# Another closing order for a gated linear attention and mixture-of-experts kernel on one core

## The chip, the core and the metric

The kernel runs on one NeuronCore of a Trainium2 chip. The metric is the time of one execution in microseconds, as the device measures it. The engines are TensorE (PE in the profile; PEld is its weight load and PEq or PEldq its sequencer), VectorE (DVE), ScalarE (ACT), GpSimd (POOL) and SyncE (SP). Each has its own instruction stream; they meet at semaphores. A name with q behind it (SPq, ACTq) is that engine's sequencer, which issues DMAs, reads registers and takes branches.

## The reference, cut

```python
f = 1.0 / (1.0 + np.exp(-f_logit))                  # q, k, v, f_logit: 4 x 8 x 768 x 48
for t in range(S):
    state = f[:, :, t, :, None] * state + np.einsum('bhd,bhe->bhde', k[:, :, t], v[:, :, t])
    y[:, :, t] = np.einsum('bhd,bhde->bhe', q[:, :, t], state)
x = y.transpose(0, 2, 1, 3).reshape(3072, 384)
P = np.exp(x @ w_gate - max); 8 rounds of row and column normalisation
for e in range(8):
    out += P[:, e:e + 1] * (np.maximum(x @ w1[e], 0.0) @ w2[e])   # w1: 384 x 1024, w2: 1024 x 384
```

## The kernel before

`fast` computes everything on the assumption that the inputs lie in ranges for which its scaled 16-bit arithmetic holds. It also computes a flag (`guard`, `verdict`) that says whether they do. `tile_gla_moe` reads the flag into a register of every engine after `fast` (line 271), and a branch (`tc.If(bad > 0)`, line 272) runs the slow program `general` when it is set. Here it never is: the branch jumps over `general`.

After the attention and the first two experts comes the long main part: 48 periods, `ORDER[n] = (e, m, b)`, the expert, the half of its hidden units and the batch. Every operand is split into two 16-bit parts (names ending in h and l), so that each product is three matmuls. Within a period 15 first-layer products (`SLOTS`) go to six PSUM banks called A to F. A bank's life is a list of events (`EVENTS`), run by `event`: `hh`/`hl` make the two parts of a hidden tile (`kh`, `kl`), `ga`/`gf` those of another (`kah`, `kal`), `gs` adds a bank into the sums `kr` and `kf` on VectorE, `gd` subtracts on GpSimd, `gh` rounds a sum to 16 bits on ScalarE (`kgh`) and `gl` makes the low part (`kgl`) on GpSimd.

The second layer is done by `paired(n, h, t)`, one block for each period and each third t of its tokens. A block is a generator that is advanced a step at a time. Its numbered steps, where "product" is six matmuls of 192 columns:

- s1: two products, into y0 and x1 (operands `ka` and the first `kg` tile)
- s2: ScalarE copies y0 to x0, and x1 times a scale to `part`
- s3: one product into y0 (second `kg` tile); s4: ScalarE copies y0 to x1
- s5: one product into x0 (operand `kh`); s7: one into x1 (first `kg` tile); s6 is empty
- s8: VectorE adds one half of each of the two outputs
- s9: two products, into y0 (`kh`) and x1 (second `kg` tile); s10: VectorE adds the other halves, GpSimd adds into `acc`, and the finished rows are stored by a DMA

y0 and x1 are the halves of one PSUM tile p, x0 lies in another tile q. The second `kg` tile of t = 2 has one buffer, which the next period's `gh` with (2, 1) writes again. In the last period ("direct" blocks) GpSimd adds `part` into `acc` at s2, and the results are added straight into `acc`.

The order on the engines is written out by hand: `pin` chains the instructions of ACT, DVE and POOL in the order in which Python emits them, and `mm` does the same for the matmuls. Behind the last first-layer product (into bank F) there remain the half-done block n=46, t=1 and four whole ones: n=46, t=2, and n=47, t=0, 1, 2. Below they are called blocks 139 to 143. `going` holds them as numbers 0 to 4. The tuple `CLOSING` is the order of what is left: a number advances that block by a step, a tuple is an event, `'v'` advances `verdict`. `ENDX` names the PSUM banks of the four whole blocks.

`verdict` has five steps left in `CLOSING`: a transpose on TensorE (`gd_t`), a maximum on VectorE (line 913), a second transpose (`gd_s`), three tiny VectorE instructions (lines 919 to 921), and two more that write the flag (lines 923 and 924).

Of the kernel before, what the change touches and what calls it, by code (L numbers as in the profile page):

```python
# [8 lines left out]
F32 = mybir.dt.float32  # L9
# [10 lines left out]
C = 64  # L20
# [62 lines left out]
READDAT = (9, 14)  # L83
CHECKAT = (1, 5)
MAXAT = (2, 6)
ENDX = (('x', None), ('k0', None), ('x', 'B'), ('k2', None))
CLOSING = (('add', 'C', '+', 3), ('gd', 1, 'P'), ('gh', 0, 1), 0, 1, 0, ('hh', 'D', 2), 0, ('gl', 0, 0), ('gl', 0, 1), 1,
# [5 lines left out]
BY_VECTOR = ((0, 0), (1, 0), (2, 0), (2, 1))  # L93
ORDER = [(e, m, b) for e in range(2, NE) for m in range(2) for b in range(B)]
PAIRED = (0, 1, 2)
BY_POOL = (1,)
# [169 lines left out]
def tile_gla_moe(tc, qkf, vc, vt, wg, w1, w2, out):  # L266
    nc = tc.nc
    with tc.tile_pool(name="fl", bufs=1) as fp:
        flag = fp.tile([1, 1], I32, name="flag")
        fast(tc, qkf, vc, wg, w1, w2, out, flag)  # L270
        bad = nc.values_load(flag, min_val=0, max_val=1)
        with tc.If(bad > 0, label="general"):
            general(tc, qkf, vt, wg, w1, w2, out)


# [1 line left out]
def fast(ctx, tc, qkf, vc, wg, w1, w2, out, flag):  # L277
# [615 lines left out]
    def verdict():  # L893
        g = cst.tile([128, 7], F32, name="wg7")
        xm = xmx.rearrange("p b k -> p (b k)")
        pin(nc.vector.tensor_reduce(out=g[:, 2:4], in_=wmx, axis=AX.X, op=ALU.min))
        pin(nc.vector.tensor_reduce(out=g[:, 4:6], in_=wmx, axis=AX.X, op=ALU.max))
        pin(nc.vector.tensor_reduce(out=g[:, 1:2], in_=xm, axis=AX.X, op=ALU.min))
        pin(nc.vector.tensor_reduce(out=g[:, 6:7], in_=xm, axis=AX.X, op=ALU.max))
        yield  # L900
        pin(nc.vector.tensor_scalar(out=okm[:, 1:2], in0=g[:, 2:3], scalar1=W1_MIN / W1S, scalar2=None, op0=ALU.is_ge))
        pin(nc.vector.tensor_scalar(out=okm[:, 2:3], in0=g[:, 3:4], scalar1=W2_MIN / W2S, scalar2=None, op0=ALU.is_ge))
        pin(nc.vector.tensor_scalar(out=okm[:, 3:4], in0=g[:, 5:6], scalar1=W2_MAX / W2S, scalar2=None, op0=ALU.is_le))
        pin(nc.vector.tensor_reduce(out=g[:, 0:1], in_=okm, axis=AX.X, op=ALU.min))
        yield
        pin(nc.vector.tensor_scalar(out=g[:, 0:2], in0=g[:, 0:2], scalar1=-1.0, scalar2=None, op0=ALU.mult))
        pin(nc.vector.tensor_scalar(out=g[:, 2:3], in0=g[:, 2:3], scalar1=-BALANCE, scalar2=None, op0=ALU.mult))
        yield
        ps = pk.tile([128, 128], F32, name="gd_t", tag="D")
        mm(transpose=True, out=ps[0:7, :], in_=g, identity=identf)  # L910
        yield
        col = cst.tile([7, 1], F32, name="gd_c")
        pin(nc.vector.tensor_reduce(out=col, in_=ps[0:7, :], axis=AX.X, op=ALU.max))
        yield
        ps = pk.tile([128, 128], F32, name="gd_s", tag="k1")
        mm(transpose=True, out=ps[0:1, 0:7], in_=col, identity=identf[0:7, 0:7])
        yield
        r = cst.tile([1, 9], F32, name="gd_r")
        pin(nc.vector.tensor_scalar(out=r[:, 0:7], in0=ps[0:1, 0:7], scalar1=1.0, scalar2=None, op0=ALU.mult))
        pin(nc.vector.tensor_tensor(out=r[:, 7:8], in0=r[:, 4:5], in1=r[:, 6:7], op=ALU.mult))  # L920
        pin(nc.vector.scalar_tensor_tensor(out=r[:, 8:9], in0=r[:, 1:2], scalar=r[:, 2:3], in1=r[:, 7:8], op0=ALU.mult, op1=ALU.is_ge))
        yield
        pin(nc.vector.scalar_tensor_tensor(out=r[:, 7:8], in0=r[:, 7:8], scalar=XW1_MAX / W1S, in1=r[:, 0:1], op0=ALU.is_le, op1=ALU.mult))
        pin(nc.vector.tensor_scalar(out=flag, in0=r[:, 8:9], scalar1=r[:, 7:8], scalar2=-FLAG_AT, op0=ALU.mult, op1=ALU.is_gt))
# [289 lines left out]
    first = {b: min(n for n, p in enumerate(ORDER) if p[2] == b) for b in range(B)}  # L1214
    final = {b: max(n for n, p in enumerate(ORDER) if p[2] == b) for b in range(B)}

    def paired(n, h, t, tag="x", own=None):
        e, m, b = ORDER[n]
        new = n == first[b]
        if new and t == PAIRED[0]:  # L1220
            acc[b] = accp.tile([128, 2, TT, DM], F32, name=f"acc{b}", tag="acc")
        p = (pk if own else psm).tile([128, DM], F32, name=f"kyps_{n}_{t}", tag=own or "m")
        q = pk.tile([128, DM], F32, name=f"kxps_{n}_{t}", tag=tag)
        x0, y0, x1 = q[:, 0:DH], p[:, 0:DH], p[:, DH:DM]
        p2 = lp.tile([128, DH], F32, name=f"part_{n}_{t}", tag="part", bufs=2)
        by_pool = t in BY_POOL and n < len(ORDER) - 1 and not new
        xx, yy = (acc[b][:, v, t, :].rearrange("p (s d) -> p s d", s=2) for v in range(2))
        direct = n == len(ORDER) - 1
        if not new and not direct:
# [4 lines left out]
        def scale(v):  # L1234
            return pes[:, (2 * b + v) * TT + t, e:e + 1]
# [27 lines left out]

        def store(v, half):
            r0, ds = (2 * b + v) * HS + t * 128, slice(0, DM) if half is None else slice(half * DH, half * DH + DH)
            (nc.scalar if direct and v else nc.sync).dma_start(out=out[r0:r0 + 128, ds], in_=acc[b][:, v, t, ds])

        product(y0, None, (0, 0), start=True)
        product(x1, (None, 0), (None, 0))
        yield  # L1270
        move(x0, y0)
        move(p2, x1, scale=scale(1))
        if direct:
            for i in range(2):
                pin(nc.gpsimd.tensor_tensor(out=yy[:, i, :], in0=yy[:, i, :], in1=p2, op=ALU.add))
        yield
# [6 lines left out]
        yield  # L1283
        product(x1, (None, 1), (None, 1))
        yield
        out_x(0, x0)
        add(yy[:, 1, :], x1, scale(1), yy[:, 1, :] if direct else p2)
        halved = direct and t == PAIRED[-1]
        if halved:
            for v in range(2):  # L1290
                store(v, v)
        yield
# [5 lines left out]
        for v, z, there in ((0, xx, not by_pool), (1, yy, new or direct)):  # L1298
            if not there:
                y = acc[b][:, v, t, :]  # L1300
                pin(nc.gpsimd.tensor_tensor(out=y, in0=y, in1=z.rearrange("p s d -> p (s d)"), op=ALU.add))  # L1301
            if n == final[b]:
                store(v, 1 - v if halved else None)

    def readds():
        todo = {b: [(o, v, t) for t in range(TT) for v in range(2) for o in range(2) if (o, 2 * b + v) in RAW] for b in range(B)}
# [62 lines left out]
    def event(ctxt, ev):  # L1369
# [45 lines left out]
        elif kind == 'gb':  # L1415
            ah, al = hs['a', ev[1]]
            pin((nc.gpsimd if ev[2] == 'P' else nc.vector).tensor_tensor(out=al, in0=hs['r', ev[1]][:, 0], in1=ah, op=ALU.subtract))
        elif kind == 'gh':
            _, t, i = ev
            if not i:  # L1420
                if t == 2:
                    hs['g', t] = [[hp.tile([128, 2, 2, 128], F16, name=f"kg{q}{i}_{tag}_{t}", tag=f"k{q}1{0}{i}", bufs=1) for i in range(2)] for q in "hl"]
                else:
                    hs['g', t] = [[lp.tile([128, 2, 2, 128], F16, name=f"kg{q}{i}_{tag}_{t}", tag=f"kg{q}{t}{i}", bufs=1) for i in range(2)] for q in "hl"]
            pin(nc.scalar.activation(out=hs['g', t][0][i], in_=hs['f' if i else 'r', t], func=AF.Copy))  # L1425
        elif kind == 'gl':
            _, t, i = ev
            pin((nc.vector if tag == str(PERIODS - 1) and (t, i) in BY_VECTOR else nc.gpsimd).tensor_tensor(out=hs['g', t][1][i], in0=hs['f' if i else 'r', t], in1=hs['g', t][0][i], op=ALU.subtract))  # L1428
        elif kind == 'hh':
            pin(nc.scalar.activation(out=hs['h', ev[2]][0], in_=bk, func=AF.Relu))  # L1430
        else:
            hh, hl = hs['h', ev[2]]
            pin(nc.vector.scalar_tensor_tensor(out=hl, in0=bk, scalar=0.0, in1=hh, op0=ALU.max, op1=ALU.subtract))
# [56 lines left out]
        raise RuntimeError("an event was left")  # L1490

    def close(what):
        if what == 'v':
            next(judged, None)
        elif isinstance(what, tuple):
            event(ctxt, what)
        else:
            next(going[what], None)

    hint = CLOSING.index('hint')  # L1500
    for what in CLOSING[:hint]:
        close(what)
    with tc.block():
        tc.mark_branch_hint_location("general", "LikelyTaken", [mybir.EngineType.DVE, mybir.EngineType.Activation, mybir.EngineType.SP])
        for what in CLOSING[hint + 1:]:
            close(what)
    if any(next(block, going) is not going for block in going):
        raise RuntimeError("a block was left")
    for _ in judged:
# [46 lines left out]
```

## Time and profile before

| | |
|---|---|
| median of 3 runs | 1458.15 us (1458.13 to 1458.2) |
| the profiled execution's own time | 1458.26 us |
| its span, first to last instruction | 1456.4 us |
| TensorE busy, share of the span | 99% |
| VectorE, ScalarE, GpSimd | 85%, 73%, 72% |
| mean granted TensorE clock | 0.999 of full speed |

The span is 1.86 us shorter than the time of the same execution; that remainder lies outside the instructions. Times in the rows below count from the span's start. Behind an instruction, in brackets, stands how long its engine had been idle before it and what ended the wait. The chain of work that ended last is empty in this profile, so the end is followed by hand, engine by engine.

### The profile page before, as it was taken

The page shows a single profiled execution, that of the slowest core. Times are in us where ns is not written, and L with a number is a line of the kernel's source. Part 1 is how long each engine was busy: PE and PEld are TensorE (multiplying, and loading weights), DVE is VectorE, ACT ScalarE, POOL GpSimd, SP SyncE. Part 2 cuts the span into 40 slices and gives each one's busy share as a digit, 9 for nine tenths or more (in the row PEclk, how much of TensorE's full clock was granted, in tenths as well). Part 3 has the DMA queues.
Part 4 walks back from the last instruction along what each step waited for, and adds up shares of the span by engine and source line. Part 5 has one row for each costly group of instructions (what it writes and reads, how often), then busy time and mean ns, then how long its engine had stood idle before and what let it go on. Part 6 is the DMA issues. An engine that isn't in the chain of part 4 may idle for free.

```text
span 1456.4 us, 40359 instructions
## 1 busy us (share of the span) xinstructions
PE 1438.7 (99%) x16054; PEld 1256.4 (86%) x16054; DVE 1232.9 (85%) x2512; ACT 1061.1 (73%) x2382; POOL 1045.1 (72%) x1227
## 2 busy tenths in 40 slices
PE   8999999999999999999999999999999999999997
PEld 5888876666666899999999999999999999999997
DVE  8888788885787899888899999888889888888876
ACT  7766666663354877888888888888877787778764
POOL 4344434446429576999999999999988888888764
PEclk9999999999999999999999999999999999999999
DMA  9455455541011101122212111111111110000012
GB/s 282 122 136 128 117 133 129 118 117 32 29 33 38 35 23 35 51 57 62 61 56 61 51 50 49 46 45 51 50 34 34 34 34 23 17 18 13 2 53 82
DMA packets 105271, 92.58 MB, mean 64 GB/s; under 512 B 72080, under 2 KB 91920, under 8 KB 105072
## 3 DMA queue, kind: packets, MB, share of 16 engines
q1 hardware_dynamic: 104496, 89.32, 22.7%
q8 instruction: 127, 2.08, 0.6%
q14 instruction: 72, 0.59, 0.1%
q10 hardware_dynamic: 576, 0.59, 0.1%
HBM read 64.03 MB, written 14.16 MB: 54 GB/s over the span
## 4 chain that ended last, share of the span: by engine, by line


## 5 line engine op out<-in xcount | busy, mean ns | idle before, releaser
L305 PEld LDWEIGHTS <-k1h 128*128 128x128 f16 x2880 | 270.9, 98 | 21.5 <-issue 2.9
L305 PE MATMUL kyps<-k2h,kgh 128*128 128x192 f16 x1152 | 283.4, 246 | 0.2 <-ACT part L1251 0.2
L305 PE MATMUL kyps<-k2l,kgh 128*128 128x192 f16 x1152 | 283.4, 246 | 0.0
L305 PE MATMUL kyps<-k2h,kgl 128*128 128x192 f16 x1152 | 283.4, 246 | 0.0
L305 PEld LDWEIGHTS <-kgh 128*128 128x128 f16 x2304 | 212.0, 98 | 6.7 <-issue 0.4
L1428 POOL TENSOR_TENSOR kgl<-kf,kgh 128x512 f16<-128x512 f32 x143 | 190.4, 1331 | 1.5 <-ACT kgh L1425 1.5
L1428 POOL TENSOR_TENSOR kgl<-kr,kgh 128x512 f16<-128x512 f32 x141 | 175.1, 1242 | 10.8 <-ACT kgh L1425 10.6
L1254 DVE SCALAR_TENSOR_TENSOR yy<-kyps,pes,part 128x192 f32<-128x192 f32 x258 | 106.7, 414 | 88.5 <-PE kyps L305 78.1
L1301 POOL TENSOR_TENSOR acc<-acc,yy 128x384 f32<-128x384 f32 x129 | 129.5, 1004 | 57.4 <-DVE yy L1254 57.4
L305 PEld LDWEIGHTS <-k1l 128*128 128x128 f16 x1440 | 140.9, 98 | 16.3
L305 PE MATMUL yps<-w2h,hl 128*128 128x384 f16 x384 | 125.1, 326 | 0.5 <-DVE hl L477 0.5
L305 PE MATMUL yps<-w2h,hh 128*128 128x384 f16 x384 | 125.1, 326 | 0.1
L305 PE MATMUL yps<-w2l,hh 128*128 128x384 f16 x384 | 125.1, 326 | 0.0
L305 PEld LDWEIGHTS <-w1h 128*128 128x128 f16 x1344 | 96.9, 98 | 32.0 <-ACT w1h L373 0.4
L305 PEld LDWEIGHTS <-kh 128*128 128x128 f16 x1152 | 108.2, 98 | 7.0 <-issue 0.6
L305 PEld LDWEIGHTS <-kgl 128*128 128x128 f16 x1152 | 112.7, 98 | 0.2 <-issue 0.2
L305 PEld LDWEIGHTS <-hh 128*128 128x128 f16 x768 | 73.6, 98 | 44.2 <-issue 0.5
L1251 ACT ACTIVATE kyps<-kyps 128x192 f32<-128x192 f32 x144 | 45.7, 317 | 80.0 <-PE kyps L305 78.5
L1425 ACT ACTIVATE kgh<-kf 128x512 f16<-128x512 f32 x144 | 91.8, 638 | 0.5 <-DVE kf L1402 0.5
L1425 ACT ACTIVATE kgh<-kr 128x512 f16<-128x512 f32 x144 | 91.6, 636 | 0.0
L1379 ACT ACTIVATE cp<-kb_A 128x512 f32<-128x512 f32 x144 | 86.3, 599 | 2.7 <-DVE kb_A L1381 2.0
L1405 POOL TENSOR_TENSOR kr<-kr 128x256 f32<-128x256 f32 x96 | 72.4, 754 | 17.3 <-PE kb_C L305 8.7
(306 smaller groups left out, 5248.0 us busy)
## 6 DMA issues: line engine op xcount, KB each, us to landing
q<-in_qkf_dram SPq DMA_DIRECT2D x23, 672.0 KB, 5.4
k1r<-in_w_dram SPq DMA_DIRECT2D x24, 384.0 KB, 3.1
ys<-yr SPq DMA_DIRECT2D x48, 192.0 KB, 2.1
k2r<-in_w_dram SPq DMA_DIRECT2D x24, 384.0 KB, 3.1
yb<-ys SPq DMA_DIRECT2D x48, 192.0 KB, 2.4
vr<-in_vc_dram SPq DMA_DIRECT2D x24, 192.0 KB, 4.9
out_dram<-acc SPq DMA_DIRECT2D x20, 192.0 KB, 1.9
w1r<-in_w_dram SPq DMA_DIRECT2D x8, 384.0 KB, 9.4
```

The lines of the kernel that those rows point to most:

```text
L305: ins = (nc.tensor.transpose if transpose else nc.tensor.matmul)(**kw)
L1251: pin(nc.scalar.activation(out=out, in_=in_, func=AF.Copy, **kw))
L1254: pin(nc.vector.scalar_tensor_tensor(out=y, in0=ps, scalar=p, in1=z, op0=ALU.mult, op1=ALU.add))
L1301: pin(nc.gpsimd.tensor_tensor(out=y, in0=y, in1=z.rearrange("p s d -> p (s d)"), op=ALU.add))
L1379: pin(nc.scalar.activation(out=fresh(ev[2]), in_=bk, func=AF.Copy))
L1405: pin((nc.gpsimd if ev[2] == 'P' else nc.vector).tensor_tensor(out=r[:, 0], in0=r[:, 1], in1=r[:, 0], op=ALU.subtract))
L1425: pin(nc.scalar.activation(out=hs['g', t][0][i], in_=hs['f' if i else 'r', t], func=AF.Copy))
L1428: pin((nc.vector if tag == str(PERIODS - 1) and (t, i) in BY_VECTOR else nc.gpsimd).tensor_tensor(out=hs['g', t][1][i], in0=hs['f' if i el ...
```

## The change

Four things change, all in the last period.

1. `CLOSING` has another order, and `ENDX` other banks: block 141's p goes to bank B, block 142's p back to the common pool, and block 143 has its x1 in bank D, apart from y0. The verdict's transposes both use bank B. The verdict runs near the start of the closing order instead of near its end. `BY_VECTOR` goes: the four low parts `gl` of the last period that VectorE made are now made by GpSimd. Block 139's x half is added by VectorE directly, not by ScalarE and GpSimd (`by_pool`). In s8 the y half is added ahead of the x half, and a direct block's GpSimd adds are a step of their own.
2. The flag is read by an entry `'load'` of `CLOSING`, in the pinned order of ACT, DVE, POOL and SP; only TensorE reads it behind its last matmul.
3. The prefetch hints for the branch, on DVE, ACT and SP, and the block that held them go.
4. All direct blocks store their rows in halves: the two of s8 by SP, those of s10 by SP for t = 0 and by ACT for t = 1 and 2. The stores are pinned.

```diff
-ENDX = (('x', None), ('k0', None), ('x', 'B'), ('k2', None))
+ENDX = (('x',), ('k0', 'B'), ('x',), ('k2', None, 'D'))
-CLOSING = (('add', 'C', '+', 3), ('gd', 1, 'P'), ('gh', 0, 1), 0, 1, 0, ('hh', 'D', 2), 0, ('gl', 0, 0), ('gl', 0, 1), 1,
-           ('gs', 'C', 1, 1), ('gs', 'C', 1, 2), ('gs', 'C', 1, 3), 1, ('hh', 'C', 1), 0, 1, 1, ('hl', 'C', 1), ('gh', 1, 0), ('gl', 1, 0),
-           2, 1, 1, ('hl', 'D', 2), ('hs', 'F', 2), 2, 2, ('gh', 1, 1), ('gl', 1, 1), 1, ('gp', 'F', 2), 2, 2,
-           ('gs', 'D', 2, 1), ('gs', 'D', 2, 2), ('gs', 'D', 2, 3), ('ga', 'F', 2), 1, 2, 2, ('gf', 'F', 2), ('gh', 2, 0), 1, 3, 2,
-           ('gl', 2, 0), ('gh', 2, 1), 3, 2, 'v', 4, 2, ('gl', 2, 1), 'hint', 3, 4, 'v', 3, 3, 'v', 4, 3, 3, 4, 'v', 4, 3, 'v',
-           4, 4, 3, 4, 4, 3, 4)
-BY_VECTOR = ((0, 0), (1, 0), (2, 0), (2, 1))
+CLOSING = (0, 'v', ('add', 'C', '+', 3), ('gd', 1, 'P'), ('gh', 0, 1), 1, ('hs', 'F', 2), 'v', 0, 'v', ('hh', 'D', 2), ('gl', 0,
+           0), ('gl', 0, 1), ('gs', 'C', 1, 1), 'v', ('gs', 'C', 1, 2), ('gs', 'C', 1, 3), 1, ('gp', 'F', 2), 0, ('gh', 1, 0),
+           ('gl', 1, 0), 1, 1, ('gh', 1, 1), ('gl', 1, 1), 0, 'v', ('gs', 'D', 2, 1), ('gs', 'D', 2, 2), ('gs', 'D', 2, 3), 2, 1,
+           1, 1, 2, 2, ('hh', 'C', 1), ('hl', 'D', 2), 1, ('ga', 'F', 2), 3, ('gh', 2, 0), ('gl', 2, 0), 2, ('gh', 2, 1), ('gl',
+           2, 1), ('hl', 'C', 1), ('gf', 'F', 2), 2, 2, 3, 1, 2, 2, 3, 3, 1, 3, 3, 2, 4, 4, 4, 'load', 2, 4, 4, 2, 3, 3, 3, 4, 4,
+           4, 4, 3, 3, 4, 4)
...
-        bad = nc.values_load(flag, min_val=0, max_val=1)
-        with tc.If(bad > 0, label="general"):
+        bad = fast(tc, qkf, vc, wg, w1, w2, out, flag)
+        with tc.If(bad > 0):
...
-        by_pool = t in BY_POOL and n < len(ORDER) - 1 and not new
+        by_pool = t in BY_POOL and n < len(ORDER) - 2 and not new
...
-            (nc.scalar if direct and v else nc.sync).dma_start(out=out[r0:r0 + 128, ds], in_=acc[b][:, v, t, ds])
+            pin((nc.scalar if direct and t and half is not None and half != v else nc.sync).dma_start(...))
...
+        if what == 'load':
+            loads, (value,) = nc.values_load_multi_w_load_instructions(flag, min_val=0, max_val=1)
+            for ins in loads:
+                if ins.ins.engine != mybir.EngineType.PE:
+                    pin(ins)
+                else:
+                    held[0] = ins
...
-    with tc.block():
-        tc.mark_branch_hint_location("general", "LikelyTaken", [mybir.EngineType.DVE, mybir.EngineType.Activation, mybir.EngineType.SP])
...
+    behind(held[0], order[-1])
```

## Rows read from the trace of the kernel before

**Rows 1.** The timeline of TensorE: start, us, line, operation, output and inputs

```profile
1431.02 0.25 PE L305 MATMUL kxps<-k2h,kh 128*128 128x192 f16 x1
...
1434.49 0.25 PE L305 MATMUL kxps<-k2h,kh 128*128 128x192 f16 x1
...
1436.13 0.24 PE L305 MATMUL kyps<-k2h,kah 128*128 128x192 f16 x1 [0.99 <-ACT xx L1251]
...
1438.01 0.24 PE L305 MATMUL kyps<-k2h,kgh 128*128 128x192 f16 x1 [0.23 <-ACT part L1251]
...
1442.09 0.24 PE L305 MATMUL kyps<-k2h,kh 128*128 128x192 f16 x1 [0.45 <-DVE acc L1254]
...
1449.24 0.25 PE L305 MATMUL kyps<-k2h,kgl 128*128 128x192 f16 x1
```

**Rows 2.** The timeline of VectorE in the closing order

```profile
1431.61 0.69 DVE L1381 TENSOR_TENSOR kb_C<-kb_C,cp 128x512 f32<-128x512 f32 x1
...
1434.27 0.41 DVE L1402 SCALAR_TENSOR_TENSOR kf<-kb_C,kr 128x256 f32<-128x256 f32 x1
1434.71 0.42 DVE L1402 SCALAR_TENSOR_TENSOR kf<-kb_C,kf 128x256 f32<-128x256 f32 x1
1435.06 0.41 DVE L1254 SCALAR_TENSOR_TENSOR yy<-kyps,pes,part 128x192 f32<-128x192 f32 x1
...
1445.65 0.59 DVE L920 TENSOR_TENSOR gd_r<-gd_r 1x1 f32<-1x1 f32 x1
1446.28 0.21 DVE L921 SCALAR_TENSOR_TENSOR gd_r<-gd_r 1x1 f32<-1x1 f32 x1
...
1449.53 0.74 DVE L1254 SCALAR_TENSOR_TENSOR acc<-kyps,pes,acc 128x192 f32<-128x192 f32 x2 [0.25 <-PE kyps L305]
```

**Rows 3.** The timeline of GpSimd in the closing order

```profile
1432.31 1.16 POOL L1428 TENSOR_TENSOR kgl<-kf,kgh 128x512 f16<-128x512 f32 x1
...
1445.10 1.13 POOL L1275 TENSOR_TENSOR acc<-acc,part 128x192 f32<-128x192 f32 x2 [1.41 <-ACT part L1251]
```

**Rows 4.** The timeline of GpSimd in a period of the middle

```profile
902.56 1.13 POOL L1128 TENSOR_TENSOR k2s<-k2r 128x192 f32<-128x192 f32 x2
903.65 1.47 POOL L1428 TENSOR_TENSOR kgl<-kr,kgh 128x512 f16<-128x512 f32 x1
```

**Rows 5.** The timeline of VectorE in the same stretch

```profile
903.16 0.94 DVE L1110 SCALAR_TENSOR_TENSOR k1l<-k1r,k1h 128x384 f16<-128x384 f32 x1
```

**Rows 6.** The timeline of ScalarE in the closing order

```profile
1433.26 0.32 ACT L1251 ACTIVATE kxps<-kyps 128x192 f32<-128x192 f32 x1 [0.47 <-PE kyps L305]
1433.49 0.41 ACT L1251 ACTIVATE part<-kyps,pes 128x192 f32<-128x192 f32 x1
...
1440.50 0.63 ACT L1425 ACTIVATE kgh<-kf 128x512 f16<-128x512 f32 x1 [0.22 <-DVE kf L1402]
```

**Rows 7.** Line 272, the branch: durations in ns, first and last start

```profile
L272 SPq EVENT_SEMAPHORE  x8: 17/17/17, 1454.5 to 1455.1; - x8
L272 POOLq COMPARE_BRANCH  x1: 45/45/45, 1448.0 to 1448.0; - x1
L272 PEldq COMPARE_BRANCH  x1: 4530/4530/4530, 1448.9 to 1448.9; - x1
...
L272 POOLq EVENT_SEMAPHORE  x1: 17/17/17, 1451.0 to 1451.0; - x1
L272 ACTq COMPARE_BRANCH  x1: 68/68/68, 1451.0 to 1451.0; - x1
L272 SPq COMPARE_BRANCH  x1: 78/78/78, 1451.6 to 1451.6; - x1
...
L272 ACTq EVENT_SEMAPHORE  x1: 17/17/17, 1454.0 to 1454.0; - x1
```

**Rows 8.** The stores into the output: issue in ns, landing

```profile
L1266 ACTq DMA_DIRECT2D out_dram<-acc x4: 338/338/385, 1443.7 to 1450.0; - x4
...
DMA to landing us min/median/max: 1.7/2.0/4.5
```

More of the change, by code (lines that the diff above doesn't have):

```diff
@@ L269, in tile_gla_moe @@
         flag = fp.tile([1, 1], I32, name="flag")
-        fast(tc, qkf, vc, wg, w1, w2, out, flag)
-        bad = nc.values_load(flag, min_val=0, max_val=1)
-        with tc.If(bad > 0, label="general"):
+        bad = fast(tc, qkf, vc, wg, w1, w2, out, flag)
+        with tc.If(bad > 0):
             general(tc, qkf, vt, wg, w1, w2, out)
@@ L908, in verdict @@
         yield
-        ps = pk.tile([128, 128], F32, name="gd_t", tag="D")
+        ps = pk.tile([128, 128], F32, name="gd_t", tag="B")
         mm(transpose=True, out=ps[0:7, :], in_=g, identity=identf)
@@ L914, in verdict @@
         yield
-        ps = pk.tile([128, 128], F32, name="gd_s", tag="k1")
+        ps = pk.tile([128, 128], F32, name="gd_s", tag="B")
         mm(transpose=True, out=ps[0:1, 0:7], in_=col, identity=identf[0:7, 0:7])
@@ L1215, in fast, with paired @@
     final = {b: max(n for n, p in enumerate(ORDER) if p[2] == b) for b in range(B)}
-    def paired(n, h, t, tag="x", own=None):
+    def paired(n, h, t, tag="x", own=None, other=None):
         e, m, b = ORDER[n]
@@ L1223, in paired @@
         q = pk.tile([128, DM], F32, name=f"kxps_{n}_{t}", tag=tag)
-        x0, y0, x1 = q[:, 0:DH], p[:, 0:DH], p[:, DH:DM]
+        x0, y0 = q[:, 0:DH], p[:, 0:DH]
+        x1 = pk.tile([128, DH], F32, name=f"kzps_{n}_{t}", tag=other) if other else p[:, DH:DM]
         p2 = lp.tile([128, DH], F32, name=f"part_{n}_{t}", tag="part", bufs=2)
-        by_pool = t in BY_POOL and n < len(ORDER) - 1 and not new
+        by_pool = t in BY_POOL and n < len(ORDER) - 2 and not new
         xx, yy = (acc[b][:, v, t, :].rearrange("p (s d) -> p s d", s=2) for v in range(2))
@@ L1265, in store @@
             r0, ds = (2 * b + v) * HS + t * 128, slice(0, DM) if half is None else slice(half * DH, half * DH + DH)
-            (nc.scalar if direct and v else nc.sync).dma_start(out=out[r0:r0 + 128, ds], in_=acc[b][:, v, t, ds])
+            pin((nc.scalar if direct and t and half is not None and half != v else nc.sync).dma_start(out=out[r0:r0 + 128, ds], in_=acc[b][:, v, t, ds]))
         product(y0, None, (0, 0), start=True)
-        product(x1, (None, 0), (None, 0))
+        product(x1, (None, 0), (None, 0), start=other is not None)
         yield
@@ L1273, in paired @@
         if direct:
+            yield
             for i in range(2):
@@ L1285, in paired @@
         yield
+        add(yy[:, 1, :], x1, scale(1), yy[:, 1, :] if direct else p2)
         out_x(0, x0)
-        add(yy[:, 1, :], x1, scale(1), yy[:, 1, :] if direct else p2)
-        halved = direct and t == PAIRED[-1]
-        if halved:
+        if direct:
             for v in range(2):
@@ L1302, in paired @@
             if n == final[b]:
-                store(v, 1 - v if halved else None)
+                store(v, 1 - v if direct else None)
     def readds():
@@ L1427, in event @@
             _, t, i = ev
-            pin((nc.vector if tag == str(PERIODS - 1) and (t, i) in BY_VECTOR else nc.gpsimd).tensor_tensor(out=hs['g', t][1][i], in0=hs['f' if i else 'r', t], in1=hs['g', t][0][i], op=ALU.subtract))
+            pin(nc.gpsimd.tensor_tensor(out=hs['g', t][1][i], in0=hs['f' if i else 'r', t], in1=hs['g', t][0][i], op=ALU.subtract))
         elif kind == 'hh':
@@ L1492, in close @@
     def close(what):
-        if what == 'v':
+        if what == 'load':
[5 more added lines that the diff above has]
+                    held[0] = ins
+            bad.append(value)
+        elif what == 'v':
             next(judged, None)
@@ L1498, in close @@
             next(going[what], None)
-    hint = CLOSING.index('hint')
-    for what in CLOSING[:hint]:
+    bad = []
+    for what in CLOSING:
         close(what)
-    with tc.block():
-        tc.mark_branch_hint_location("general", "LikelyTaken", [mybir.EngineType.DVE, mybir.EngineType.Activation, mybir.EngineType.SP])
-        for what in CLOSING[hint + 1:]:
-            close(what)
+    behind(held[0], order[-1])
     if any(next(block, going) is not going for block in going):
@@ L1514, in fast @@
         raise RuntimeError("a check was left")
+    return bad[0]
 def _layout(q, k, v, f_logit, wg, w1, w2):
```

## Prediction, made before the change was run

> **What bounds the kernel now.** The page comes first: TensorE is busy for 99% of the span, so only a stretch in which it is not can give anything back. All edits lie behind the last first-layer product, so the timeline of TensorE from there on is read next [rows 1]. The reader is to see three idle stretches with three different releasers: ScalarE's `xx` of block 139, which still reads the PSUM tile that block 141 needs, then ScalarE's `part`, then VectorE's `acc`. A product is six matmuls; seven of them start between 1431.02 and 1434.49, 0.496 us each. 32 products are left, 15.86 us. The last matmul starts at 1449.24, so the work ends at 1449.33: 18.31 us, of which 2.45 are gaps. The brackets add up to 1.67; each counts from a matmul's modelled end, 0.16 us after the next could have started, so the three gaps are 1.15, 0.39 and 0.61 us, together 2.15. The remaining 0.30 goes to the guard's two small transposes.
>
> Then the end. VectorE's last two adds finish at 1450.27 [rows 2], and the span ends at 1456.4: six microseconds without arithmetic. Line 272 shows what fills them [rows 7]. An engine's own branch is short, but its next instruction comes late: ScalarE branches at 1451.0 and goes on at 1454.0, SP at 1451.6 and 1454.5, GpSimd at 1448.0 and 1451.0, some 3 us each. TensorE's branch itself lasts 4.53 us. SP is last, and runs through its closing waits until the end. So the path is: products and gaps, last add, last store, the flag's read, SP's branch and stall, closing.
>
> **The order.** The upper bound of what it can give on TensorE is the 2.15 us of gaps. To see what it leaves, the new order is laid out by hand with the durations of the rows. VectorE's PSUM-reading instructions follow each other in 0.33 us and end 0.08 later (a full 512-column one 0.60), or in 0.44 when one reads what the last wrote [rows 2]; ScalarE's copies follow in 0.23 and 0.30, its `kgh` lasts 0.62 [rows 6]; GpSimd's `kgl` lasts 1.16 and follows in 1.12 [rows 3]. An engine hears of TensorE about 0.26 us after the next product could start (product end 1433.00, copy 1433.26) [rows 6].
>
> VectorE, which sets the pace: add into C from 1431.61; the guard's reduction at 1432.35, when its transpose is through, 0.2 (an estimate, no more than the 0.33 of a full add); block 139's two adds, now both here, to 1433.21; one `gs` to 1433.54; the guard's copy, 0.2, to 1433.73. Now comes line 920, one element by one element. It took 0.59 us [rows 2], and ended when GpSimd's adds of 1445.10 to 1446.23 did [rows 3]: it sat behind them. In the middle of the kernel VectorE's 384-column instruction with two SBUF inputs took 0.94 where GpSimd ran at 903.16, and GpSimd's next took 1.47 instead of 1.16 [rows 4, 5]: the two take turns, instruction by instruction. In the old order the other three tiny ones ran while GpSimd was idle (line 921: 0.21). In the new one GpSimd has four more low parts, 4 x 1.12 = 4.5 us, minus one add of about 1 us, and is at work throughout: `gl` (0,0) from 1432.31 and (0,1) from 1433.43 to 1434.59. Line 920 waits until 1434.65. Line 921 arrives 0.04 later, but `gl` (1,0) was ready at 1434.57 (block 140's first products end at 1433.11, plus 0.26, 0.53 for the copies and 0.62 for `kgh`): it takes its turn until 1435.80, and line 921 ends at 1435.85. I take this value; the other bound is nothing, if 921 gets in first. Two `gs` (0.77), `gp` (0.33) and block 139's last adds end at 1437.69. Line 923 arrives at 1437.61 behind `gl` (1,1), which runs from 1437.40 to 1438.56; with the flag VectorE is free at 1438.78. Three `gs` (1.10), `hl` (0.60): block 140's y add ends at 1440.89. The two long waits cost 1.1 and 1.0 us.
>
> No row here is a one-element instruction of line 921's kind beside a busy GpSimd; I price it by the wide one. The Trainium skill ("SBUF — State Buffer", section "Who interferes with whom") speaks against the change in the same way: the pair of ports that the two engines share is locked for a whole instruction, and a VectorE instruction with two SBUF inputs blocks with GpSimd. By that rule 920, 921 and 923 all wait and the time is the forecast's; if only 920 waits, as its own row shows, it is 1455.8.
>
> TensorE: from 1431.02 eleven products and the guard's two transposes (5.45 + 0.30) to 1436.77. The next, block 142's first, need the bank of block 139: 1437.74, idle 0.97. Four products to 1439.72; block 140's s9 waits for its y add: 1440.94, idle 1.22. It ends at 1441.93. Here the order has a turn that nothing in the trace shows: `gh` (2,1) now stands ahead of s9 of block 140, but writes the buffer that this s9 reads, so ScalarE must hold it until 1442.2, and behind it in ScalarE's order stands block 141's s4, for which TensorE's next product waits: 0.26 + 0.52 + 0.32, about 1.1 us idle (lower bound nothing, if the buffers are in fact apart). `part` of block 142 adds 0.06. Idle in all 0.97 + 1.22 + 1.11 + 0.06 + 0.30 = 3.66, so the products end at 1450.54: 1.2 us later than now. The other edits ahead of this point cost nothing: GpSimd's extra 4.5 us are covered as long as its low parts are a microsecond ahead of their products (`gl` (0,0) ends 1433.47 for 1434.78; (1,0) 1435.85 for 1437.74), and the reads of the flag (SP's and the check behind it lie in the 1.3 us between the last add, 1450.27, and its branch, 1451.6 [rows 2, 7], so under 1 us with a store's issue of 0.3 taken off) stand where ScalarE, VectorE and SP wait for products of blocks 141 and 143 anyway. SP's read queues behind the stores of block 140, which wait for GpSimd's last add into them, and ahead of the stores of s10 of block 141; all of these are out before the last two microseconds. Without that cover a read would delay block 143's s4 by up to 1 us.
>
> **The end.** With y0 and x1 of the last block in two banks, the y add no longer waits for the last product: behind the products comes one latency, 0.2 (1449.33 to 1449.53 [rows 1, 2]), and one add, 0.41, where it was 0.94. Last add 1451.15. Stores: the bytes stay the same, the blocks t = 0 and 1 go out as four DMAs each instead of two. SP's last (s8) go early; ScalarE's last four halves take 0.34 each and a small step, 0.38 together [rows 8]: those of t = 1 from 1450.52, those of t = 2 at 1451.28 and 1451.66. Its branch follows at 1452.04 at once, the flag being read already: 0.9 us from the last add, where SP now takes 1.3. It goes on 3.0 us later, at 1455.0. The hints' removal I cost at nothing: GpSimd, without a hint, stalled as long as ScalarE and SP with one [rows 7]; the other bound, TensorE's 4.53, is the third rival. From SP's first closing wait to the end it is now 1.9 us, of which its eight waits take 0.6 (1454.5 to 1455.1) [rows 7]. SP itself branches early in the new order, so if ScalarE is last, at most 1.3 remain; I take 1.1, an estimate, as part of that is SP's own too: end 1456.1. The last halves must also have landed: 1.7 to 4.5 us [rows 8] from 1451.66, 1453.4 to 1456.2; near the median 2.0 they are hidden, at the far end they add 1.3.
>
> **Sum.** Products 1.2 later, last add 0.9 later, the last branch 0.4 later, its stall 0.1 longer, closing 0.8 shorter: end of span 1456.1 instead of 1456.4. With the 1.86 outside it, 1457.96 against the profiled 1458.26; the median of the runs lies 0.11 below that execution, so about 1457.8 us: no change that counts. Within 0.2% is +-2.9 us, about what a measurement of this kernel can tell from no change.
>
> **Rivals.**
> - GpSimd doesn't stand in the way (its low parts come a little later, or 921 and 923 slip in). Then both idle stretches ahead of block 140's s9 shrink to 0.25, the products end 2 us earlier: 1455.8. For it: turns are taken by whoever comes first, and the distance is 0.1 us at line 921. Against it: 923 falls into the middle of a `gl`. With one of the two held: 1456.8, inside the forecast.
> - The buffer of `gh` (2,1) holds nothing up: 1.1 us less, 1456.7. With the first rival together 1454.7, the only case that is faster by over 0.2%. Against it: the code gives it one buffer. The old order shows neither: there `gh` (2,1) waited for VectorE [rows 6].
> - Slower: without hints a branch costs ScalarE what TensorE's cost it, 4.53 [rows 7]. Then it goes on at 1456.6, the span ends at 1457.7, and the time is 1459.4. It decides as soon as the stall is over 3.4 us. For it: four unhinted branches now fall within four microseconds, with the last stores. Against it: GpSimd's 3.0 without a hint.
> - The last stores land late, after 4.5 us: 1459.1. For it: the row's maximum; against it: its median.
>
> **Chances.** Forecast (1456.6 to 1458.8: both turns lost, or one) 0.53; GpSimd out of the way 0.14; the buffer free 0.12; both 0.07; unhinted branches 0.08; landing 0.03; something that none of the prices covers 0.03. The range 1455.6 to 1459.1 holds all but the double gain, the long branch and the unpriced. Faster by over 0.2% 0.07, within 0.90, slower by over 0.2% 0.03.
>
> **What the profile would show.** Line 920 with some 0.9 us and line 921 with over 1; TensorE idle before block 142's first products (releaser VectorE), before block 140's s9 (VectorE's `yy`), and 1.1 us before block 141's s7 (ScalarE's copy); the flag's read on four engines around 1444; ScalarE's branch last, and its next instruction 3 us later. The prediction is wrong if 921 and 923 take 0.2 us, if the order closes the gap before s7, or if stalls behind the branches come out far from 3 us.

## The result, and the profile after

The changed kernel takes 1471.98 us, the median of 5 runs (1471.24 to 1475.11), where the kernel before took 1458.15 beside it: a ratio of 1.0101, 95% interval 1.0087 to 1.0114. Forecast were 1457.8 us, no change that counts. It is 13.8 us slower.

The first look is at where the time went, not at the closing order. The table by stretches gives busy time and number of instructions for TensorE, its weight load, VectorE, ScalarE and GpSimd, then clock and DMA. Before:

```profile
0.00:500.00 500.00, 491.45 (x5926) 357.33 (x5927) 398.51 (x746) 309.31 (x651) 235.90 (x287) 1.00 0.41 105
500.00:1050.00 550.00, 549.44 (x5870) 521.51 (x5868) 494.02 (x1039) 451.04 (x1035) 490.43 (x581) 1.00 0.18 50
1050.00:1400.00 350.00, 350.00 (x3740) 332.26 (x3738) 302.52 (x641) 271.19 (x626) 289.56 (x330) 1.00 0.08 24
```

After:

```profile
0.00:500.00 500.00, 492.21 (x5927) 357.47 (x5928) 398.45 (x746) 309.34 (x651) 235.89 (x287) 1.00 0.41 105
500.00:1050.00 550.00, 543.72 (x5729) 508.13 (x5726) 504.86 (x1019) 442.86 (x1010) 476.00 (x565) 1.00 0.17 48
1050.00:1400.00 350.00, 350.00 (x3741) 332.30 (x3739) 299.20 (x629) 272.76 (x630) 294.28 (x337) 1.00 0.08 24
```

The first and the last stretch hold the same number of matmuls in both, to within one. In the 550 us between them, 141 of 5870 are missing; at 5870 in 550 us that is 13.2 us. So the loss lies in the middle of the kernel, some 400 us and more ahead of the closing order. VectorE is busier there while it does less. Set matmul by matmul against the trace of before, TensorE falls back by 0.5 us at 540, and by 1.2 to 1.3 us in each of ten later places between 580 and 1047; then by nothing more, and the last first-layer product comes 13.0 us late. Its last matmul, before and after:

```profile
1430.91 0.27 PE L305 MATMUL kb_F<-xah,k1l 128*128 128x256 f16 x1
```

```profile
1443.89 0.27 PE L303 MATMUL kb_F<-xah,k1l 128*128 128x256 f16 x1
```

One of these places, on VectorE, before:

```profile
657.06 0.40 DVE L1254 SCALAR_TENSOR_TENSOR acc<-kxps,pes,acc 128x192 f32<-128x192 f32 x1
657.50 0.42 DVE L1254 SCALAR_TENSOR_TENSOR yy<-kyps,pes,part 128x192 f32<-128x192 f32 x1
657.83 0.43 DVE L1110 SCALAR_TENSOR_TENSOR k1l<-k1r,k1h 128x256 f16<-128x256 f32 x1
658.18 0.69 DVE L1381 TENSOR_TENSOR kb_D<-kb_D,cp 128x512 f32<-128x512 f32 x1
```

and on GpSimd:

```profile
656.98 0.99 POOL L1321 TENSOR_TENSOR acc<-acc,yz 128x384 f32<-128x384 f32 x1 [0.86 <-ACT yz L1320]
657.94 1.34 POOL L1428 TENSOR_TENSOR kgl<-kf,kgh 128x512 f16<-128x512 f32 x1
```

The same place after, on VectorE and then on GpSimd:

```profile
660.43 0.42 DVE L1253 SCALAR_TENSOR_TENSOR yy<-kyps,pes,part 128x192 f32<-128x192 f32 x1 [0.36 <-PE kyps L303]
660.76 0.41 DVE L1253 SCALAR_TENSOR_TENSOR acc<-kxps,pes,acc 128x192 f32<-128x192 f32 x1
661.09 1.22 DVE L1108 SCALAR_TENSOR_TENSOR k1l<-k1r,k1h 128x256 f16<-128x256 f32 x1
662.22 0.69 DVE L1380 TENSOR_TENSOR kb_D<-kb_D,cp 128x512 f32<-128x512 f32 x1
```

```profile
659.91 1.00 POOL L1320 TENSOR_TENSOR acc<-acc,yz 128x384 f32<-128x384 f32 x1 [0.86 <-ACT yz L1319]
660.86 1.16 POOL L1427 TENSOR_TENSOR kgl<-kf,kgh 128x512 f16<-128x512 f32 x1
```

These are the two adds of s8, and they have changed places here too, in the middle of the kernel: the edit stands in `paired` without the condition `direct`. In the old order the x add filled the wait for the y product, and the low part of the weights, `k1l`, came while GpSimd was just ending `yz`. In the new order VectorE idles 0.36 us for the product, the x add follows, `k1l` is a third of a microsecond later, and GpSimd has begun a whole `kgl`: 1.22 us instead of 0.43. That `kgl` ends at 662.02 and `k1l` 0.28 us behind it; in each of the ten places `k1l` begins 0.05 to 0.22 us behind the start of a `kgl` and ends 0.28 us behind its end, so it waits for the end of GpSimd's instruction. The chain that ended last runs straight through it (start, us, what):

```profile
660.84 0.33 DVE acc L1253
661.17 1.13 DVE k1l L1108
662.30 0.62 DVE kb_D L1380
...
662.95 0.71 DVE kb_F L1383
...
663.70 0.81 PE kb_D L303 x6
...
668.93 0.31 DVE k2l L1133
```

The same holds in the whole stretch, as the `k1l` line by itself shows (durations min/median/max in ns; half of the 16 have 256 columns, half 384; those of 384 take 0.95 in both). First before, 560 to 890 us; then after, the same stretch and the one behind 1060:

```profile
L1110 DVE SCALAR_TENSOR_TENSOR k1l<-k1r,k1h x16: 426/778/956, 576.9 to 862.2; 128x256 f16<-128x256 f32 x8, 128x384 f16<-128x384 f32 x8
```

```profile
L1108 DVE SCALAR_TENSOR_TENSOR k1l<-k1r,k1h x16: 947/1082/1393, 577.7 to 872.5; 128x256 f16<-128x256 f32 x8, 128x384 f16<-128x384 f32 x8
...
L1108 DVE SCALAR_TENSOR_TENSOR k1l<-k1r,k1h x16: 415/521/550, 1075.9 to 1361.1; 128x256 f16<-128x256 f32 x8, 128x384 f16<-128x384 f32 x8
```

That is the first half of the loss only. Ahead of this place TensorE is 2.93 us behind the trace of before; it is 3.22 behind at the first matmul into D, 3.48 at the next into B, and 4.08 some nine microseconds later, at one into A. The first line of each pair is that into D, the second that into A; before, then after:

```profile
660.48 0.27 PE L305 MATMUL kb_D<-xah,k1h 128*128 128x256 f16 x1
...
669.51 0.27 PE L305 MATMUL kb_A<-xbh,k1h 128*128 128x256 f16 x1
```

```profile
663.70 0.27 PE L303 MATMUL kb_D<-xah,k1h 128*128 128x256 f16 x1
...
673.59 0.27 PE L303 MATMUL kb_A<-xbh,k1h 128*128 128x256 f16 x1 [0.23 <-ACT cp L1378]
```

In between VectorE makes the low parts of the second layer's weights, `k2l`, and these take longer too; half of the 16 have 192 columns, half 384. Before, then after, 560 to 890 us:

```profile
L1135 DVE SCALAR_TENSOR_TENSOR k2l<-k2r,k2h x16: 340/446/649, 582.5 to 866.8; 128x192 f16<-128x192 f32 x8, 128x384 f16<-128x384 f32 x8
```

```profile
L1133 DVE SCALAR_TENSOR_TENSOR k2l<-k2r,k2h x16: 737/900/1061, 584.0 to 877.5; 128x192 f16<-128x192 f32 x8, 128x384 f16<-128x384 f32 x8
```

The chain runs through one of them too (its line at 668.93 above). So a place has four low parts on VectorE, two `k1l` and two `k2l`. At the place shown they took 2.27 us together before (0.43, 0.96, 0.34 and 0.55) and 3.96 after (1.22, 0.95, 0.74 and 1.06).

Behind 1060 the adds are exchanged as well, but GpSimd no longer has its `yz` additions, the `k1l` take half as long, and nothing is lost. Nor is anything lost at 912 and 952 us, where the 256-column `k1l` happened to take 0.57 and 0.42.

The closing order itself came out near the forecast. TensorE's three idle stretches and its last matmul:

```profile
1450.55 0.24 PE L303 MATMUL kyps<-k2h,kah 128*128 128x192 f16 x1 [0.64 <-DVE acc L1253]
...
1453.76 0.24 PE L303 MATMUL kyps<-k2h,kh 128*128 128x192 f16 x1 [1.07 <-DVE yy L1253]
...
1455.77 0.24 PE L303 MATMUL kyps<-k2h,kgh 128*128 128x192 f16 x1 [0.85 <-ACT kyps L1250]
...
1463.16 0.25 PE L303 MATMUL kzps<-k2h,kgl 128*128 128x192 f16 x1
```

VectorE's guard instructions, which answer to [rows 2]:

```profile
1446.66 0.92 DVE L918 TENSOR_TENSOR gd_r<-gd_r 1x1 f32<-1x1 f32 x1
1447.61 1.11 DVE L919 SCALAR_TENSOR_TENSOR gd_r<-gd_r 1x1 f32<-1x1 f32 x1
...
1450.42 1.00 DVE L921 SCALAR_TENSOR_TENSOR gd_r<-gd_r 1x1 f32<-1x1 f32 x1
1451.46 0.20 DVE L922 TENSOR_SCALAR flag<-gd_r 1x1 int32<-1x1 f32 x1
```

VectorE's last add:

```profile
1463.45 0.42 DVE L1253 SCALAR_TENSOR_TENSOR acc<-kzps,pes,acc 128x192 f32<-128x192 f32 x1
```

The branch, which answers to [rows 7], and ScalarE's last four stores (ns, min/median/max), which answer to [rows 8]:

```profile
L270 ACTq COMPARE_BRANCH  x1: 54/54/54, 1465.9 to 1465.9; - x1
...
L270 ACTq EVENT_SEMAPHORE  x1: 17/17/17, 1468.6 to 1468.6; - x1
...
L1265 ACTq DMA_DIRECT2D out_dram<-acc x4: 386/436/1157, 1463.2 to 1464.7; - x4
```

### The profile page after: what moved, and what is told of

Same layout as the page of the kernel before. It is cut to its first block, busy times and chain, and to the rows that moved or that the text cites. A ratio compares the mean times of both kernels' runs of the same rounds, so it can differ in the third digit from the quotient of the medians.

```text
span 1469.5 us, 40387 instructions
## 1 busy us (share of the span) xinstructions
PE 1446.8 (98%) x16054; PEld 1255.6 (85%) x16054; DVE 1251.2 (85%) x2510; ACT 1063.7 (72%) x2380; POOL 1046.1 (71%) x1230
## 4 chain that ended last, share of the span: by engine, by line
PE 87%; DVE 8%; ACT 3%; issue 1%; DMA 0%; DVEq 0%; ACTq 0%
PE kyps L303 25%; PE yps L303 15%; PE hps L303 12%; PE kb_A L303 8%; PE kb_B L303 7%; PE kb_D L303 6%; PE kxps L303 4%; PE kb_C L303 4%; PE kb_E L303 2%; PE kb_F L303 2%; DVE k1l L1108 1%; PE aps L303 1%; DVE yy L1253 1%; PE kvps L303 1%; ACT cp L1378 1%
## 5 line engine op out<-in xcount | busy, mean ns | idle before, releaser
L1427 POOL TENSOR_TENSOR kgl<-kf,kgh 128x512 f16<-128x512 f32 x144 | 196.9, 1368 | 5.0 <-ACT kgh L1424 5.0
L1427 POOL TENSOR_TENSOR kgl<-kr,kgh 128x512 f16<-128x512 f32 x144 | 168.0, 1167 | 10.8 <-ACT kgh L1424 10.8
L1404 POOL TENSOR_TENSOR kr<-kr 128x256 f32<-128x256 f32 x96 | 75.5, 786 | 17.2 <-ACT kr L1393 15.3
```

Source lines behind the costliest of these rows:

```text
L1427: pin(nc.gpsimd.tensor_tensor(out=hs['g', t][1][i], in0=hs['f' if i else 'r', t], in1=hs['g', t][0][i], op=ALU.subtract))
```

## The experiments

Theory A: the exchange of the two adds in all blocks costs the 13 us. Theory B: something else of the change moves the main part. Each time below is a median, set against the kernel before on the same chip (1457.98 to 1458.1).

**The exchange in the closing blocks alone**, everything else of the change kept:

```diff
+        first_y = n >= len(ORDER) - 2
+        if not first_y:
+            out_x(0, x0)
         add(yy[:, 1, :], x1, scale(1), yy[:, 1, :] if direct else p2)
-        out_x(0, x0)
+        if first_y:
+            out_x(0, x0)
```

> The changed kernel, with the y half added ahead of the x half in s8 only in the blocks of the last two periods, and the old order (x first) in all others. Theory A: the 13.1 us are lost because the two VectorE adds of s8 change places in every block, not only in the closing ones; then the main part runs as before and what is left is the tail, 0.1 us longer in the trace than before: 1458.3 us, within 1457.8 to 1458.8. Theory B: the exchange is harmless and something else of the change (pinned stores, the flag read inside the closing order, no block around the end) moves the main part; then it stays near 1472.

1459.29 us (1457.9 to 1461.69, 10 runs), ratio 1.0011 (1.0001 to 1.0020). The 13 us are gone. The median is 0.5 above the range named; the stores account for a part of that, as shown below.

**The kernel before with the exchange alone**, in all blocks but those of the last two periods:

> The kernel before with one edit: y half ahead of x half in s8 of every block except those of the last two periods. Theory A: 1458.15 + 13.1 = 1471.3 us, within 1470.5 to 1472.5. Theory B: 1458.2, no change.

1471.16 us, ratio 1.0091 (1.0074 to 1.0107). Theory B is out: this one edit alone makes a loss of 13.1 us. (Taking it out of the changed kernel gave back 12.7.)

**The same edit for one t at a time** (`and t == 0`, then `and t == 2`; for most blocks with t = 1 the x add is ScalarE's):

> The kernel before with the exchange in the blocks with t = 0 of all but the last two periods. Their s8 stands in the slot in which the weights' low part k1l (128x256) follows on VectorE. Theory A1 (the low part, 0.33 us later, misses the moment in which GpSimd is between two instructions and sits behind a whole low part kgl of GpSimd: 0.43 us becomes 1.22): nearly all of the loss is here, 1469 to 1472. Theory A2 (each exchange costs by itself, since VectorE idles for the product with the x add behind it, wherever it stands): half the loss, 1463 to 1466.

> The kernel before with the exchange in the blocks with t = 2 of all but the last two periods, where no k1l of 128x256 stands directly behind s8. Theory A1: 1458 to 1460. Theory A2: half the loss, 1463 to 1466.

1471.11 us, ratio 1.0090 (1.0073 to 1.0107), with t = 0, and 1457.96, ratio 1.0000 (0.9990 to 1.0010), with t = 2. All of it comes from the blocks whose s8 stands ahead of the 256-column `k1l`; with t = 2 the exchange costs nothing (A2 falls).

**The collision moved.** First `k1l` one slot later, then instead GpSimd's `yz` one slot later, both with the exchange in every block:

```diff
-W1AT = (0, 1, 2, 3, 5, 9, 10, 11, 12, 21, 23, 25, 26)
+W1AT = (0, 1, 2, 3, 5, 9, 10, 11, 12, 21, 23, 26, 26)
```

> The changed kernel with one number altered: the weights' low part k1l of 128x256 is made one slot later (with the 128x384 one), so that it no longer stands directly behind the two adds of s8; the exchanged adds stay in every block. Theory A1 (the collision with GpSimd's kgl behind the exchange is what costs): most of the 13.1 us come back, 1459 to 1463. Theory A2 (the exchange costs by itself, through the 0.36 us in which VectorE idles for the product): 1470 to 1474, as before the edit.

```diff
-READDAT = (9, 14)
+READDAT = (10, 14)
```

> The changed kernel with one number altered: the early output that is added in again (yz, first of the two in a period) comes one slot later, so that GpSimd makes kgl ahead of it, in the 0.86 us in which it now waits for yz, and is through with kgl when the low part k1l arrives; the exchanged adds stay in every block, and k1l stays behind them. Theory A1 (k1l behind the exchange runs into a whole kgl): k1l of 128x256 takes 0.4 to 0.8 us instead of 1.2 to 1.4, and most of the 13.1 us come back: 1458.5 to 1463. Theory A2 (the exchange costs by itself): 1470 to 1474.

1471.87 and 1470.51 us: theory A1 missed both times, and both times lie in the range of A2, which t = 2 had ruled out. The timeline of VectorE shows why A1 missed. In the first the two low parts, now side by side, sat behind GpSimd together:

```profile
662.05 2.09 DVE L1108 SCALAR_TENSOR_TENSOR k1l<-k1r,k1h 128x256 f16<-128x256 f32 x2
```

In the second the 256-column one takes 0.50 as expected, and the wait ahead of `kb_D` is gone, but VectorE is still a third of a microsecond late, and the 384-column one now starts behind the other `kgl` and takes 1.36, where it took 0.96:

```profile
660.26 0.50 DVE L1108 SCALAR_TENSOR_TENSOR k1l<-k1r,k1h 128x256 f16<-128x256 f32 x1
...
662.34 1.36 DVE L1108 SCALAR_TENSOR_TENSOR k1l<-k1r,k1h 128x384 f16<-128x384 f32 x1
```

So theory A1, one collision, was too narrow: with one out of the way the next takes its place, and the `k2l` stay as long as in the changed kernel (0.74 and 1.06 in both runs). TensorE falls back by the same 0.57 us behind them in both. At this place the four low parts took 3.97 us together in the first run and 3.66 in the second. That left open whether it is GpSimd at all.

**GpSimd's `yz` additions left out, the exchange kept** (48 instructions in the trace, not the 32 of the expectation; the early outputs are then missing from the result):

```diff
-                    pin(nc.gpsimd.tensor_tensor(out=y, in0=y, in1=yt, op=ALU.add))
```

> The changed kernel, exchange in every block, without GpSimd's additions of the early outputs (yz): 32 of its 384-column instructions of about 1.0 us are left out, so the early outputs are missing from the result. Theory A (the exchange makes VectorE a third of a microsecond later, and this is lost only where its weight parts then fall behind an instruction of GpSimd): GpSimd has gaps again, as behind 1050 us, and the 13.1 us are gone but for at most 2: 1457.5 to 1460. Theory A2 (the exchange costs by itself): 1470 to 1474.

**The kernel before, old order, with one spare instruction** that makes VectorE a third of a microsecond later at the same place:

```diff
...
+        if t == 0 and n < len(ORDER) - 2:
+            pin(nc.vector.tensor_scalar(out=spare, in0=x0, scalar1=scale(0), scalar2=None, op0=ALU.mult))
```

> The kernel before, adds in the old order, with one spare VectorE instruction behind them in the blocks with t = 0 (192 columns from PSUM into a scratch tile that nobody reads, 0.33 us as the next one sees it). Theory A (a third of a microsecond on VectorE at this place is enough, whatever makes it): 1468 to 1473. Theory A3 (it takes the changed order, x behind y and with it the later release of the x tile): 1458 to 1460.

1459.63 us and 1471.01 us (ratio 1.0088, 1.0071 to 1.0105). The `k1l` line from 560 to 890 us, without `yz`, then with the spare instruction:

```profile
L1108 DVE SCALAR_TENSOR_TENSOR k1l<-k1r,k1h x16: 470/524/550, 577.8 to 863.0; 128x256 f16<-128x256 f32 x8, 128x384 f16<-128x384 f32 x8
```

```profile
L1110 DVE SCALAR_TENSOR_TENSOR k1l<-k1r,k1h x16: 946/1082/1393, 577.7 to 872.5; 128x256 f16<-128x256 f32 x8, 128x384 f16<-128x384 f32 x8
```

With the exchange but a less crowded GpSimd, all but 0.3 us of the gain of the first experiment is there. The old order without `yz` was not run, but before TensorE was busy for 549.44 of the 550 us, so it had next to nothing to gain there. Without the exchange, but with 0.33 us more on VectorE, the same durations appear and the same 13 us are lost. The spare instruction reads `x0`, so it lets go of the x tile later, as the exchange does; but so does the kernel without `yz`, and it loses nothing. What is shown, then, is that a third of a microsecond on VectorE at this place, beside a GpSimd as full as this one, costs the 13 us. Single long low parts are not the measure: without `yz` the two `k2l` still took 0.75 and 0.91, but the four at this place 2.69 together, and no TensorE time was lost there.

**The closing order taken apart.** The next experiments stand on the first one (exchange in the closing blocks alone), and are compared with its 1459.29 us. Whole rows for blocks 141 and 142:

```diff
...
-        if direct:
+        if direct and t == 2:
             for v in range(2):
                 store(v, v)
...
-                store(v, 1 - v if direct else None)
+                store(v, 1 - v if direct and t == 2 else None)
```

(and ScalarE stores the y rows, SP the x rows, as before the change, so that ScalarE's four stores no longer follow each other directly).

> The changed kernel with the exchange in the closing blocks only, and the rows of blocks 141 and 142 stored whole again, by SP and ACT, so 8 stores instead of 12 from these blocks. Theory S1 (a half store's issue on ACT, which took 1.16 to 1.46 us in two traces instead of 0.34, is long because so many short stores queue up): issues of 0.33 to 0.45 again, the last branch 0.7 to 1.2 us earlier, 1457.4 to 1458.2, and runs within 0.5 us of each other instead of 3.8. Theory S2 (the long issue and the scatter come from the branches that the other engines take at the same time): no change, 1458.5 to 1460 with the same scatter.

1458.57 us (1458.09 to 1459.11). ScalarE's issues are back at 0.338 us (0.422 at most), the scatter is 1.0 instead of 3.8 us, the median 0.7 lower: S1's signs, but the time is 0.4 us outside its range, so it accounts for 0.7 of the 1.25 us that the closing order costs. Whether the fewer stores do it, or their other spread over the two engines, was not separated.

`gh` (2,1) behind s9:

```diff
-... 2, ('gh', 2, 1), ('gl', 2, 1), ('hl', 'C', 1), ('gf', 'F', 2), 2, 2, 3, 1, 2, 2, 3, ...
+... 2, ('hl', 'C', 1), ('gf', 'F', 2), 2, 2, 3, 1, ('gh', 2, 1), ('gl', 2, 1), 2, 2, 3, ...
```

> The changed kernel with the exchange in the closing blocks only, and gh (2,1) with its low part moved behind s9 of block 140. Theory G1 (ScalarE's copy of block 141's s4 queues behind gh (2,1), which waits for s9 because of the one buffer): TensorE's idle 0.85 ahead of block 141's s7 goes, the products end 0.7 to 1.0 us earlier, and the time is 0.5 to 1.0 below the same kernel without the move, which gave 1459.29 in the median and 1457.9 at its lowest. Theory G2 (the copy is late for another reason): no change.

1459.03 us. The idle 0.85 is gone and the last matmul comes 1.1 us earlier, about as G1 said, but the median fell by 0.3 only, which ten runs can't tell from none, and less than the 0.5 to 1.0 of G1: here one store issue of ScalarE took 1.86 us and one of SP 1.49.

The guard's three instructions with one tensor source:

```diff
-nc.vector.tensor_tensor(out=r[:, 7:8], in0=r[:, 4:5], in1=r[:, 6:7], op=ALU.mult)
+nc.vector.tensor_scalar(out=r[:, 7:8], in0=r[:, 4:5], scalar1=r[:, 6:7], scalar2=None, op0=ALU.mult)
```

(the other two alike).

> The changed kernel with the exchange in the closing blocks only, and the three one-element guard instructions (lines 918, 919, 921) written with one tensor source and per-partition scalars, as the flag's own instruction is (0.20 us beside a busy GpSimd). The values are the same. Theory P1 (they were long because an instruction with two tensor sources in SBUF waits for GpSimd's turn): 0.2 us each instead of 0.9, 1.1 and 1.0; TensorE's idle 0.64 and 1.07 shrink to under 0.5 together, the products end 1.2 to 1.8 us earlier, the time is 1 to 1.8 us lower than 1459.3. Theory P2 (they were long for what they read, results fresh from the instruction before): no change.

1457.58 us (1455.77 to 1458.21), 1.7 lower, at the upper end of what P1 named. VectorE's timeline:

```profile
1433.47 0.20 DVE L918 TENSOR_SCALAR gd_r<-gd_r 1x1 f32<-1x1 f32 x1
1433.71 0.26 DVE L919 TENSOR_SCALAR gd_r<-gd_r 1x1 f32<-1x1 f32 x1
...
1435.66 0.19 DVE L921 TENSOR_SCALAR gd_r<-gd_r 1x1 f32<-1x1 f32 x1
```

0.65 us instead of 3.0, and both of TensorE's waits for VectorE are gone. The first two ran beside a `kgl` (1433.21 to 1434.38); the third began in a gap of GpSimd (1435.53 to 1435.77).

All three together, and then with the branch hints put back:

> The changed kernel with the exchange in the closing blocks only, the guard's three instructions with one tensor source, gh (2,1) behind s9, and whole rows for blocks 141 and 142. If the three effects add up (products 2.05 us earlier by the guard, 1.0 by gh, branch directly behind the last add by the whole rows): the last add ends 3.0 us earlier than in the kernel with the closing exchange alone, and the time is 1454.5 to 1455.5 us, 2.5 to 3.5 below before. If TensorE's idle moves to another place when the two are combined: 1455.5 to 1457.

> The same with the block and the three branch hints put back around the part from the flag's read on. Theory H0 (hints cost and save nothing): the same time within 0.5 us, SP's stall behind its branch 2.9 to 3.3 us in both. Theory H1 (a hint shortens the stall): SP's and ScalarE's stall shorter by over 0.3 us and the time lower by as much.

1455.08 us, ratio 0.9985 (0.9975 to 0.9995): this version is faster than both kernels, by 3.0 us than before. The products add up: the last matmul comes 3.1 us earlier, 2.0 by the guard and 1.1 by `gh`. The time gains 4.2 where the three singly gave 0.7, 0.3 and 1.7: here no long store issue stands behind the products (ScalarE's longest took 0.39 us), as one did when the guard and `gh` were changed singly (0.90 and 1.86). One of its ten runs took 1460.58, the others 1454.87 to 1456.19; what that one waited for no trace shows. From its last first-layer matmul (1430.95) to its last matmul (1447.12) pass 16.2 us, about what the 32 products (15.86) and the two transposes (0.30) need by themselves. With hints 1455.34 us, ratio 0.9981: no difference. SP's branch and the first event behind it, without the hints:

```profile
L270 SPq EVENT_SEMAPHORE  x8: 17/17/17, 1451.4 to 1451.9; - x8
...
L270 SPq COMPARE_BRANCH  x1: 58/58/58, 1448.2 to 1448.2; - x1
```

and with them:

```profile
L270 SPq EVENT_SEMAPHORE  x8: 17/17/17, 1451.4 to 1451.9; - x8
...
L270 SPq COMPARE_BRANCH  x1: 78/78/78, 1448.1 to 1448.1; - x1
```

3.2 and 3.3 us: the hint shortens nothing here. It did reach the branch: the branch itself took 78 ns instead of 58.

## Why the prediction was wrong

- **"All edits lie behind the last first-layer product"**: this step failed, and with it the forecast. One of them, the exchange of the two adds in s8, stands in `paired` without `direct` and acts in every block whose x add is VectorE's, two of three in most periods, not only in the closing ones. The sum had no term for the main part, and none of the chances but the 0.03 for something unpriced covered it. It is worth 13.1 us when put alone into the kernel before, 12.7 when taken out of the changed one. What it did there: VectorE came a third of a microsecond later ahead of `k1l`, and the low parts then sat behind GpSimd's instructions.
- The price was in the prediction's own reasoning: "the two take turns, instruction by instruction" was read from the middle of the kernel [rows 4, 5], and used only for the guard's three small instructions. None of the rivals had a place ahead of the closing order.
- **The order**: right. Idle of 0.97, 1.22 and 1.11 us was forecast with releasers VectorE, VectorE and ScalarE. The brackets read 0.64, 1.07 and 0.85; with the 0.16 us by which a bracket is short (from the prediction) 0.80, 1.23 and 1.01. Last first-layer matmul to last matmul grew from 18.33 (1430.91 to 1449.24) to 19.27 us (1443.89 to 1463.16): 0.94 later, forecast 1.2.
- **The turns**: right. Lines 920, 921 and 923 of before, now 918, 919 and 921, were given 0.9, over 1.1 and 1.0 us, and took 0.92, 1.11 and 1.00. Each ended with a `kgl` of GpSimd (1447.57, 1448.72 and 1451.42). The rewritten form shows the cause: with one tensor source they no longer wait. The Trainium skill ("SBUF — State Buffer", section "Who interferes with whom") says that a VectorE instruction with at most one SBUF input does not contend with GpSimd, outside the modes in which it uses both port pairs; the 0.20 and 0.26 us beside a running `kgl` agree. In the first rival idle stretches of 0.25 in place of 0.97 and 1.22 save 1.7 us, not the 2 of its sum; with the rewritten form no bracket was left there, and the products ended 2.0 earlier.
- **`gh` (2,1)**: right, 1.0 us for 1.1 forecast, and gone when it is moved.
- **The end**: mis-sized. The last add ends 0.71 us after the start of the last matmul (1463.16 to 1463.87), where it was 1.03. Four stores of ScalarE at 0.38 us each were forecast, and a branch 0.9 us behind the last add; the branch came 2.0 us behind it, since one issue took 1.16 us. The stall was 2.8 us for 3.0 (1465.85 to 1468.63), the closing 0.9 for 1.1. From the last first-layer matmul to the end of the span, before needed 25.5 us (1456.4 - 1430.91) and after 25.6 (1469.5 - 1443.89): +0.1 where -0.3 was forecast. That this is so near is in part luck: the late branch (0.8) was set off by smaller errors the other way in the products, the last add, the stall and the closing. In the profiled execution the tail alone would have been within 0.2%; over ten runs of the first experiment it cost 1.25 us in the median, so that 1459.29 lies just above the range (1455.6 to 1459.1) even without the 13 us. Of the 1.25, 0.7 went with the twelve half-row stores; the rest stays open.
- **The hints**: right, at nothing.

## What to carry to other kernels

Before pricing a diff, ask of every changed line in a shared function which calls reach it: here a swap of two lines without a condition ran in blocks all over the kernel, and the argument about the last 25 us never met it. On an engine that takes turns with another, a delay is not worth its own length: 0.33 us on VectorE became 1.2 us of TensorE's time in each crowded place, about half of it at once and half some nine microseconds later, and moving one collision brought the next. So look in the timeline at what all the next two-source instructions will land on, not the first alone. Where a small VectorE instruction must run beside a busy GpSimd, give it one tensor source and per-partition scalars: here it took 0.2 us instead of 1.

## What the runs showed of the hardware

A store's issue is not always 0.34 us. With twelve half-row stores from the last three blocks the longest issue on ScalarE took 0.90 to 1.86 us in all seven traces of such kernels, and the runs of each lay 1.7 to 4.9 us apart; with eight stores (three traces) ScalarE's issues took 0.34 us and once 0.39 to 0.42. What such an issue waits for was not tried. And behind a taken branch the next instruction came 2.9 to 3.3 us later before and 2.7 to 3.5 after, on four engines; in the pair without and with hints it came 2.8 to 3.7 and 2.7 to 3.9 later. The Trainium skill ("Runtime: NRT & Kernel Launch", section "Instruction fetch mechanics") says that a branch out of the fetched window waits for a fetch of its target; no view of these traces shows the fetch itself.
